# An mLSTM, mixture-of-experts and dense kernel on Trainium2: the tokens of the first three chunks are routed as one table

## The chip, the cores and the metric

The kernel runs on one core of a Trainium2 chip. The metric is device time in microseconds (us), the median of three runs. In the rows PE is the tensor engine, DVE the vector engine, ACT the scalar engine, POOL the GpSimd engine and SP the engine that issues most of the transfers.

## What is computed

Three layers in a row. The first is a gated recurrence over 768 steps for 4 batches and 8 heads of 40 columns. Its output is read as 3072 tokens of 320 columns. The second layer sends each token to the one of 8 experts with the largest logit and scales the expert's output by two gates. The third is a plain two-matrix layer. Cut to what matters:

```python
for t in range(S):                                     # attention, per batch and head
    m_new = np.maximum(f_gate[:, :, t] + m, i_gate[:, :, t])
    C = f_stab * C + i_stab * np.einsum('bhd,bhe->bhde', vt, kt)
    y[:, :, t] = o * h_tilde / denom
...
logits = x @ w_gate                                    # experts, x is (3072, 320)
e_idx = np.argmax(logits, axis=1)
gate_w = probs[np.arange(N), e_idx]
eom = 1.0 / (1.0 + np.exp(-(x @ w_output_gate)))
for e in range(E):
    mask = e_idx == e
    ye = np.maximum(x[mask] @ w1[e], 0.0) @ w2[e]
    out[mask] = gate_w[mask, None] * eom[mask, e, None] * ye
...
h = x @ w_in                                           # dense layer
g = np.maximum(0.01 * h, h)
return g @ w_out
```

## The kernel before

The recurrence is worked in chunks: 6 chunks of 128 steps by 4 batches give 24 units, unit c*4 + b. A hand-written loop (`for i in range(n_units)`) takes one unit further per iteration. The list `steps` (lines 426 to 441) sets what an iteration does and for which unit: an entry (lag, function) runs the function for unit i - lag. The order of this list is the order of the instructions on PE, ACT, DVE and POOL; each of these works its own queue strictly in that order.

The steps that matter here, with the names of the rows:

- `stage_d` (lag 0): PE makes the decay exponents pd (L278), ACT the exponentials pe (L287), four of eight from each of two PSUM banks. `stage_m` (lag 1): POOL masks pe to the lower triangle (L292).
- `stage_s` (lag 1): PE makes the scores psc (L317, 16 matmuls), DVE multiplies them with pe into ww (L324).
- `stage_o` (lag 2): PE makes pin (L338), the state update pu (L354) and ppv (L375); DVE makes the start of hh (L345), adds pu to the state st (L371), adds ppv to hh (L378) and makes the denominator from it (L382 to L384). `stage_g` (lag 3): POOL multiplies the output gate o with hh (L388) and masks the state into stm (L390). `stage_v` (lag 1): POOL scales v into wv (L306), not in the last chunk. `stage_y` (lag 3): DVE makes y (L402).
- `router.front` and `router.logits` (lag 5): PE transposes y (rt, L592), ACT copies it (xt, L594), PE multiplies with the two gates' weights (L602), ACT copies the 16 logits into the table lg (L603).
- `router.pick` (lag 6) works once per chunk, on the table of its four units: eight DVE operations (L629 to L636) find the largest logit and the one-hot oh. `router.rank` (lag 6) counts with small PE matmuls into the bank pp (L648, L649, L653) how many earlier tokens went to each expert, and ACT makes two exponentials (L660, L661). `router.place` (lag 7) makes from pp and the running count (both 8 numbers wide per unit) the slot sl of each token and its scale in the table meta: nine DVE operations (L671 to L683), ten for chunk 3 (L685).
- `router.scatter` (lag 0, last in the iteration): for a unit in the queue that `place` fills, POOL zeroes one number (gap, L696) and issues an indirect DMA (L697) that writes the unit's 128 rows of meta to the slots. Before the last chunk it takes one unit per iteration, in the last chunk four. When the last unit of chunk 3 has gone, the slots are loaded for the first half of the first expert (L1172), and POOL gathers its tokens (xr0a, L1014).

All eight PSUM banks come from one pool of eight, taken in turn. An iteration takes eight banks, rt, two pd, two psc, pin, pu and ppv, and a ninth, pp, where a table is ranked. A bank is taken by a new tile when the last reader of the old one is done.

At the end of iterations 5, 9, 13, 17 and 21 ACT opens the output gates of the next chunk with a sigmoid (L127), between two loads of its function table. Behind the loop the last units, chunks 4 and 5 of the table and the first expert's beginnings are interleaved by hand. Then come the experts and, from about 405 us on, the dense layer.

Of the kernel before, what the change touches and what calls it, by code (L numbers as in the profile page):

```python
# [10 lines left out]
F32 = mybir.dt.float32  # L11
F32R = mybir.dt.float32r
BF16 = mybir.dt.bfloat16
I32 = mybir.dt.int32
# [5 lines left out]
P = 128  # L20
B, H, S, D = 4, 8, 768, 40
BH = B * H
NC_ = S // P
DM = H * D
# [4 lines left out]
E = 8  # L29
# [8 lines left out]
NBIG = 3  # L38
CAPS = (CAP,) * (NBIG + 1) + (CAP - P,) * (E - NBIG - 1)
NOVER = 32  # L40
WARM = (11, 12, 7)
PW = 1024
SP = (mybir.EngineType.SP,)
# [11 lines left out]
def apart(tc, inst, before, why):  # L55

    for p in before:
        tc.declare_no_dep(inst.ins, p.ins, reason=why)
    before.append(inst)


def keep_warm(nc, psum, t, n):

    pt = psum.tile([P, 512], F32, tag="ps", name="warm")
    for _ in range(n):
        nc.tensor.matmul(pt, t[:, 0:P], t[:, 0:512], start=True, stop=True)
# [8 lines left out]
def attention(ctx, tc, qT, kT, k, v, i_gate, f_gate, o_gate, psum, ident, router, side, feed, fill):  # L75
    nc = tc.nc
    ctx.enter_context(tc.manual_schedule(engines=ORDERED))
    apool = ctx.enter_context(tc.tile_pool(name="apool", bufs=1))
    lpool = ctx.enter_context(tc.tile_pool(name="lpool", bufs=2))
    spool = ctx.enter_context(tc.tile_pool(name="spool", bufs=3))  # L80
    wpool = ctx.enter_context(tc.tile_pool(name="wpool", bufs=2))

    def ps(name):
# [64 lines left out]
    for j in range(3):  # L148
        nc.gpsimd.affine_select(
            sel, sel, pattern=[[-1, BH]], compare_op=ALU.not_equal, fill=1.0, base=-BH * j, channel_multiplier=1  # L150
        )

    m = apool.tile([BH, S], F32, name="m")
# [254 lines left out]
    for t in st:  # L408
# [4 lines left out]
        rowm, rowm, pattern=[[-D, 3]], compare_op=ALU.is_ge, fill=0.0, base=0, channel_multiplier=1  # L413
    )
    nc.gpsimd.affine_select(
        rowm, rowm, pattern=[[D, 3]], compare_op=ALU.is_ge, fill=0.0, base=D - 1, channel_multiplier=-1
# [3 lines left out]
    for i in range(3, AHEAD):  # L420
# [17 lines left out]
        (2, stage_o),  # L438
        (6, router.rank),
        (5, router.logits),  # L440
        (0, lambda c, b: router.scatter(B if c == NC_ - 1 else 1)),
    ]
    for i in range(n_units):
        for lag, fn in steps:
# [20 lines left out]
    a, b, c, d = units[-4:]  # L465
# [51 lines left out]
class Router:  # L517
# [39 lines left out]
    def setup(self):  # L557
        nc, cp = self.nc, self.cp
        self.tri = cp.tile([P, P], BF16, name="tri")
        nc.gpsimd.memset(self.tri, 1.0)  # L560
        nc.gpsimd.affine_select(
            self.tri, self.tri, pattern=[[1, P]], compare_op=ALU.is_gt, fill=0.0, base=0, channel_multiplier=-1
        )
        self.desc = cp.tile([P, E], F32, name="desc")
        nc.gpsimd.iota(
            self.desc, pattern=[[-REG, E]], base=E * REG, channel_multiplier=0, allow_small_or_imprecise_dtypes=True
        )
        self.meta = cp.tile([P, NC_, B, 4], I32, name="meta")
        nc.gpsimd.iota(self.meta, pattern=[[P, NC_], [S, B], [0, 4]], base=0, channel_multiplier=1)
        self.order.setup()  # L570

    def clear(self):
# [5 lines left out]
        ]  # L578

    def sink(self, c, b):  # L580
        if b == 0:
            self.lg[c] = self.rp.tile([P, B, 2 * E], F32, tag="lg", name=f"lg{c}")
        self.y[c, b] = self.rp.tile([P, DM], F32, tag="y", name=f"y{c}_{b}", bufs=4)
        return self.y[c, b].rearrange("p (h d) -> p h d", d=D)

    def front(self, c, b):
# [10 lines left out]
    def logits(self, c, b, copy=None):  # L597
        nc = self.nc
        pl = self.pl
        for kt in range(3):  # L600
            for t in HALVES:
                nc.tensor.matmul(pl[t], self.xt[:, kt, t], self.wg[:, kt], start=(kt == 0), stop=(kt == 2))  # L602
        (copy or nc.scalar.copy)(self.lg[c][:, b], pl)  # L603

    def span(self, c, b):

        if c == NC_ - 1:
            return {B // 2 - 1: (0, B // 2), B - 1: (B // 2, B // 2)}.get(b, (0, 0))
        return (0, B) if b == B - 1 else (0, 0)

    def t3(self, name, n, dt=F32):
        return self.rp.tile([P, B, E], dt, tag=name, name=name)[:, :n]

    def t2(self, name, n, dt=F32):
        return self.rp.tile([P, B], dt, tag=name, name=name)[:, :n]

    def pick(self, c, b):
        b0, n = self.span(c, b)
        if not n:
            return  # L620
        nc = self.nc
        lg = self.lg[c][:, b0 : b0 + n]
        g, og = lg[:, :, 0:E], lg[:, :, E : 2 * E]
        bc = lambda a: a[:, :, None].to_broadcast([P, n, E])
        desc = self.desc[:, None, :].to_broadcast([P, n, E])
        mx, eq = self.t2("mx", n), self.t3("eq", n)
        r, oh = self.t2("r", n), self.t3("oh", n, BF16)
        ex, zs = self.t3("ex", n), self.t2("zs", n)
        nc.vector.reduce_max(mx, g, axis=AX.X)  # L629
        nc.vector.tensor_tensor(eq, g, bc(mx), ALU.is_equal)  # L630
        nc.vector.tensor_mul(eq, eq, desc)
        nc.vector.reduce_max(r, eq, axis=AX.X)
        nc.vector.tensor_tensor(oh, desc, bc(r), ALU.is_equal)
        nc.vector.tensor_sub(ex, g, bc(mx))
        nc.vector.tensor_mul(eq, oh, og)
        nc.vector.reduce_sum(zs, eq, axis=AX.X)  # L636
        self.picked[c, b] = r, oh, ex, zs
# [25 lines left out]
    def place(self, c, b):  # L663
        b0, n = self.span(c, b)
        if not n:
            return
        nc = self.nc
        r, oh, ex, zs = self.picked.pop((c, b))
        pos, pr, se = self.t3("pos", n), self.t2("pr", n), self.t2("se", n)
        sl = self.t2("sl", n, I32)  # L670
        nc.vector.tensor_add(  # L671
            pos,
            self.pp[:, : n * E].rearrange("p (b e) -> p b e", e=E),
            self.base[:, None, :].to_broadcast([P, n, E]),
        )
        nc.vector.tensor_mul(pos, pos, oh)
        nc.vector.reduce_sum(pr, pos, axis=AX.X)
        nc.vector.scalar_tensor_tensor(sl, pr, float(E * REG), r, ALU.add, ALU.subtract)
        nc.vector.reduce_sum(se, ex, axis=AX.X)
        nc.vector.tensor_scalar(zs, zs, 1.0, None, ALU.add)  # L680
        nc.vector.scalar_tensor_tensor(se, se, 1e-9, zs, ALU.add, ALU.mult)
        nc.vector.reciprocal(self.meta[:, c, b0 : b0 + n, 2].bitcast(F32), se)
        nc.vector.tensor_add(self.base, self.base, self.pp[:, n * E : (n + 1) * E])  # L683
        if c == NC_ - 3:
            nc.vector.tensor_max(self.base, self.base, self.bump)  # L685
        self.queue += [(c, b0 + i, sl[:, i : i + 1]) for i in range(n)]

    def scatter(self, most=B):
        for c, b, sl in [self.queue.pop(0) for _ in range(min(most, len(self.queue)))]:
# [4 lines left out]
    def scatter_one(self, c, b, sl):  # L694
        nc = self.nc
        nc.gpsimd.memset(self.gap, 0)  # L696
        put = nc.gpsimd.indirect_dma_start(  # L697
            out=self.slots,
            out_offset=bass.IndirectOffsetOnAxis(ap=sl, axis=0),
            in_=self.meta[:, c, b, :],  # L700
            in_offset=None,
        )
        apart(self.tc, put, self.puts, "every token has a slot of its own")


class Order:


    def __init__(self, nc, pool):
# [6 lines left out]
        self.total = pool.tile([P, 1], I32, name="total")  # L716
        self.rows = pool.tile([P, NOVER], I32, name="rows")
        self.owner = pool.tile([P, NOVER], I32, name="owner")

# [30 lines left out]
    def past(self, pool):  # L750

        v = self.nc.vector
        wd = [P, NOVER, E]
        one = lambda nm: pool.tile([P, E], F32, name=nm, bufs=1)
        cap, nt, ends, ones = one("cap"), one("nt"), one("ends"), one("ones8")
        ni = pool.tile([P, E], I32, name="ni", bufs=1)
        steps = pool.tile([P, NOVER], F32, name="steps", bufs=1)
        d, ind, t = (pool.tile(wd, F32, name=nm, bufs=1) for nm in ("past_d", "past_i", "past_t"))

        def shares():  # L760
            self.nc.gpsimd.iota(
                steps, pattern=[[1, NOVER]], base=0, channel_multiplier=0, allow_small_or_imprecise_dtypes=True
            )
# [375 lines left out]
def mlstm_moe_mlp(  # L1139
# [48 lines left out]
    with ExitStack() as actx:  # L1188
# [39 lines left out]
        side += [nop] * 6 + parts  # L1228
        side += [nop, both(*acts[0:2]), acts[2], nop, acts[3], both(*acts[4:6]), acts[6]]
        attention(tc, qT, kT, k, v, i_gate, f_gate, o_gate, psum, ident, router, side, feed, fill)  # L1230
        load_slots(0, NJ // 2, NJ)

    wslot.append(ctx.enter_context(tc.tile_pool(name="wslot1", bufs=1)))
    with ExitStack() as mctx:
# [16 lines left out]
        loads = [w[0] for w in wide]  # L1251
        keep_warm(nc, psum, wts[0].w1h[:, 0], WARM[0])
        xs = ex.x(xr, "0b").all()
        for e in range(E):
# [63 lines left out]
            if e == E - 2:  # L1318
                more = nc.values_load(order.total[0:1, 0:1], min_val=0, max_val=NOVER)
            gs = []  # L1320
# [16 lines left out]

    keep_warm(nc, psum, wts[E].w1h[:, 0], WARM[1])
    with ExitStack() as octx:
# [21 lines left out]
    ctx.enter_context(tc.manual_schedule(engines=ORDERED))  # L1361
    keep_warm(nc, psum, wts[E].w1h[:, 0], WARM[2])
    for f in range(4):
# [98 lines left out]
```

## Time and profile before

| | us |
|---|---|
| median of three runs | 757.37 |
| the three runs | 756.65, 757.37, 759.11 |
| the profiled execution, its own time | 756.48 |
| its span | 754.8 |
| PE busy in the span | 720.6 (95%) |
| DVE, ACT, POOL busy | 461.5, 357.0, 353.2 |

The span is the time between the first and the last instruction of the profiled execution; the rest of its time lies around it. The busy times are sums over three layers with different limits, so they don't say what any one of them waits for.

### The profile page before, as it was taken

The numbers are of one execution on the slowest core, as the hardware profiler recorded it, in microseconds if no ns is written. First come the engines' busy times: TensorE is split into PE (matmuls) and PEld (weight loads), VectorE is DVE, ScalarE is ACT, GpSimd is POOL, SyncE is SP. The second block draws the span as 40 slices with busy tenths as digits, with TensorE's granted clock in tenths as the row PEclk, the third lists the DMA queues.
The fourth block names the chain that finished last, engine by engine and source line by source line (L and its number), as shares of the span: only waits on it lengthen the run. The fifth ranks groups of instructions, "written<-read, shape, count | busy, mean of one in ns | idle before, by whom it ended". The sixth has DMA issues, their size and how long they took to land.

```text
span 754.8 us, 14574 instructions
## 1 busy us (share of the span) xinstructions
PE 720.6 (95%) x5450; PEld 668.7 (89%) x5450; DVE 461.5 (61%) x925; ACT 357.0 (47%) x803; POOL 353.2 (47%) x396
## 2 busy tenths in 40 slices
PE   8888998899999999899998999999999999999998
PEld 6888998788879889799997988988988988988998
DVE  8989989674569889866764758048048038037020
ACT  5678776632562643554465355045045046046041
POOL 8757788754236473553322346046046036037041
PEclk9999999999999999999999999999999999999999
DMA  6887886411986766765762011001001000000000
GB/s 169 248 243 186 227 225 160 116 63 37 320 253 209 248 242 183 267 213 194 203 195 66 1 53 36 27 9 36 27 10 34 29 9 19 27 10 0 27 11 17
DMA packets 61791, 87.69 MB, mean 116 GB/s; under 512 B 8396, under 2 KB 53464, under 8 KB 60440
## 3 DMA queue, kind: packets, MB, share of 16 engines
q1 hardware_dynamic: 55928, 67.43, 30.2%
q10 hardware_dynamic: 2336, 10.75, 4.1%
q0 software_dynamic: 3456, 8.58, 3.5%
q8 instruction: 43, 0.70, 0.4%
q14 instruction: 28, 0.23, 0.1%
HBM read 67.87 MB, written 19.51 MB: 116 GB/s over the span
## 4 chain that ended last, share of the span: by engine, by line
PE 60%; DVE 11%; DMA 10%; issue 9%; POOL 5%; ACT 3%; POOLq 0%; SPq 0%; ACTq 0%; DVEq 0%
PE p L990 23%; PE po L1001 9%; PE po L999 9%; PE po L1000 9%; DMA xr<-xd,ms 7%; PE psc L317 4%; PE ppv L375 2%; POOL xr L1014 2%; DMA r<-in_moe_w_dram 2%; PE pd L278 1%; POOL x L1061 1%; PE pu L354 1%; PE rt L592 1%; DVE ww L324 1%; DVE w2l L907 1%
## 5 line engine op out<-in xcount | busy, mean ns | idle before, releaser
L1379 POOL TENSOR_TENSOR g2l<-lk,g2h 128x512 fp32r<-128x512 f32 (+1 forms) x112 | 126.6, 1133 | 213.7 <-ACT g2h L1378 203.7
L1388 DVE TENSOR_TENSOR lk<-p,lk 128x512 f32<-128x512 f32 (+1 forms) x112 | 68.9, 615 | 181.1 <-ACT lk L1387 179.1
L990 PE MATMUL p<-xhm,w1h 128*128 128x512 f32 (+1 forms) x336 | 119.5, 359 | 0.0
L990 PE MATMUL p<-xhm,w1l 128*128 128x512 f32 (+1 forms) x336 | 119.2, 359 | 0.0
L1001 PE MATMUL po<-w2h,g2l 128*128 128x320 f32 x384 | 118.7, 309 | 0.0
L1000 PE MATMUL po<-w2l,g2h 128*128 128x320 f32 x384 | 118.7, 309 | 0.0
L999 PE MATMUL po<-w2h,g2h 128*128 128x320 f32 x384 | 118.6, 309 | 0.0
L1387 ACT ACTIVATE lk<-p 128x512 f32<-128x512 f32 (+1 forms) x112 | 60.1, 536 | 73.7 <-PE p L990 73.7
L1061 POOL DMA_INDIRECT x<-yo,ms x26 | 32.1, 1236 | 104.0 <-ACT yo L1055 103.4
L990 PE MATMUL p<-xlm,w1h 128*128 128x512 f32 (+1 forms) x224 | 80.5, 359 | 0.1
L1000 PEld LDWEIGHTS po<-w2l,g2h 128*128 128x128 f32 x384 | 72.1, 188 | 0.2
L999 PEld LDWEIGHTS po<-w2h,g2h 128*128 128x128 f32 x384 | 72.1, 188 | 0.2
L1001 PEld LDWEIGHTS po<-w2h,g2l 128*128 128x128 f32 x384 | 72.1, 188 | 0.0
L1402 ACT COPY yo<-po 128x320 f32<-128x320 f32 x24 | 10.2, 426 | 130.7 <-PE po L1001 130.7
L990 PEld LDWEIGHTS p<-xhm,w1l 128*128 128x128 f32 x336 | 63.5, 189 | 9.4
L990 PEld LDWEIGHTS p<-xhm,w1h 128*128 128x128 f32 x336 | 63.4, 189 | 9.4
L1001 PE MATMUL po<-w2h,gl 128*128 128x320 f32 x208 | 64.9, 312 | 1.3 <-DVE gl L1041 1.3
L999 PE MATMUL po<-w2h,gh 128*128 128x320 f32 x208 | 65.4, 314 | 0.0
L1000 PE MATMUL po<-w2l,gh 128*128 128x320 f32 x208 | 64.7, 311 | 0.0
L1378 ACT CAST g2h<-lk 128x512 fp32r<-128x512 f32 (+1 forms) x112 | 61.6, 550 | 1.6 <-DVE lk L1388 1.6
L952 DVE STREAM_TRANSPOSE xtm<-x2r 32x384 f32<-32x384 f32 (+3 forms) x144 | 59.6, 414 | 2.8
L990 PE MATMUL ph<-xh,w1h 128*128 128x384 f32 (+1 forms) x168 | 60.8, 362 | 0.0
(251 smaller groups left out, 1597.9 us busy)
## 6 DMA issues: line engine op xcount, KB each, us to landing
r<-in_moe_w_dram SPq DMA_DIRECT2D x6, 1280.0 KB
r<-in_moe_w_dram SPq DMA_DIRECT2D x7, 1024.0 KB
raw<-in_moe_w_out_dram ACTq DMA_DIRECT2D x5, 1024.0 KB
r<-in_moe_w_dram SPq DMA_DIRECT2D x16, 256.0 KB
raw<-in_moe_w_in_dram ACTq DMA_DIRECT2D x4, 1024.0 KB
v<-in_v_dram SPq DMA_DIRECT2D x24, 164.0 KB
o<-in_o_gate_dram SPq DMA_DIRECT2D x6, 640.0 KB
k<-in_k_dram SPq DMA_DIRECT2D x24, 160.0 KB
```

The source lines that it names most:

```text
L317: nc.tensor.matmul(psc[:, j * P : (j + 1) * P], w["kTm"][:, h], w["qT"][:, h // 3], start=True, stop=True,)
L375: nc.tensor.matmul(ppv[t, h * VW : (h + 1) * VW], w["ww"][:, h, t], vb[:, h], start=True, stop=True)
L952: self.nc.vector.transpose(out=xt[f, k].rearrange("p k (j t) -> p k j t", t=P)[:, :, :, t], in_=blocks[t, :, g].rearrange("p j k f -> p k ...
L990: nc.tensor.matmul(ps, a, b, start=(i == 0), stop=(i == len(seq) - 1))
L999: nc.tensor.matmul(ps, gh[:, js], wh, start=(f == 0), stop=False)
L1000: nc.tensor.matmul(ps, gh[:, js], wl, start=False, stop=False)
L1001: nc.tensor.matmul(ps, gl[:, js], wh, start=False, stop=(f == n - 1))
L1061: put = self.nc.gpsimd.indirect_dma_start(out=self.x2, out_offset=bass.IndirectOffsetOnAxis(ap=ms[:, j, 1:2], axis=0), in_=yo, in_offset=None,
L1378: nc.scalar.copy(gh, lk)
L1379: nc.gpsimd.tensor_sub(gl, lk, gh.bitcast(F32))
L1387: nc.scalar.activation(lk, pf, AF.Copy, scale=0.01)
L1388: nc.vector.tensor_max(lk, pf, lk)
```

## The change

The new table GROUPED lists five groups of units: the twelve units of chunks 0 to 2, the four of chunk 3, the four of chunk 4, and two halves of chunk 5. `pick`, `rank` and `place` work once per group, when its last unit has come. So the calls for chunk 0 (i = 9 and 10) and chunk 1 (i = 13 and 14) are gone, and those at i = 17 and 18, where chunk 2 stood, work on twelve units. The number of scatters in an iteration is set anew too: one up to chunk 3, two in chunk 4's iterations (16 to 19), four in the last chunk's. The wide table and what is worked out from it have one buffer; y has three buffers for four, and the pool of hh two for three. The functions keep their code otherwise; lines move down by one to ten.

The diff, cut to its core:

```diff
+GROUPED = ((0, 3 * B), (3 * B, B), (4 * B, B), (5 * B, B // 2), (5 * B + B // 2, B // 2))
...
-    spool = ctx.enter_context(tc.tile_pool(name="spool", bufs=3))
+    spool = ctx.enter_context(tc.tile_pool(name="spool", bufs=2))
...
-        (0, lambda c, b: router.scatter(B if c == NC_ - 1 else 1)),
+        (0, lambda c, b: router.scatter({NC_ - 1: B, NC_ - 2: 2}.get(c, 1))),
...
-        self.meta = cp.tile([P, NC_, B, 4], I32, name="meta")
+        self.meta = cp.tile([P, NC_ * B, 4], I32, name="meta")
...
     def sink(self, c, b):
-        if b == 0:
-            self.lg[c] = self.rp.tile([P, B, 2 * E], F32, tag="lg", name=f"lg{c}")
-        self.y[c, b] = self.rp.tile([P, DM], F32, tag="y", name=f"y{c}_{b}", bufs=4)
+        b0, n = self.group(c, b)
+        if c * B + b == b0:
+            size = (B, 2) if n <= B else (n, 1)
+            self.lg[b0] = self.rp.tile([P, size[0], 2 * E], F32, tag=f"lg{size[0]}", name=f"lg{b0}", bufs=size[1])
+        self.y[c, b] = self.rp.tile([P, DM], F32, tag="y", name=f"y{c}_{b}", bufs=3)
...
+    def group(self, c, b):
+
+        for first, n in GROUPED:
+            if first <= c * B + b < first + n:
+                return first, n
 
     def span(self, c, b):
-
-        if c == NC_ - 1:
-            return {B // 2 - 1: (0, B // 2), B - 1: (B // 2, B // 2)}.get(b, (0, 0))
-        return (0, B) if b == B - 1 else (0, 0)
+        first, n = self.group(c, b)
+        return (first, n) if c * B + b == first + n - 1 else (0, 0)
 
     def t3(self, name, n, dt=F32):
-        return self.rp.tile([P, B, E], dt, tag=name, name=name)[:, :n]
+        m = max(n, B)
+        return self.rp.tile([P, m, E], dt, tag=f"{name}{m}", name=name, bufs=2 if m == B else 1)[:, :n]
...
-        lg = self.lg[c][:, b0 : b0 + n]
+        lg = self.lg[b0][:, 0:n]
...
-        self.queue += [(c, b0 + i, sl[:, i : i + 1]) for i in range(n)]
+        self.queue += [((b0 + i) // B, (b0 + i) % B, sl[:, i : i + 1]) for i in range(n)]
```

How this moves instructions is shown at two places. In these rows a number behind a name tells its buffer, and the brackets what an instruction waits for. The first place is DVE's queue in iteration 9, from the denominators to ww. Before:

```order
L384 RECIPROCAL ppv_2_1009<-ppv_2_1009 128x8
L629 TENSOR_REDUCE mx<-lg_489 128x4
L630 TENSOR_TENSOR eq<-lg_489,mx 128x32
L631 TENSOR_TENSOR eq<-eq,desc 128x32
L632 TENSOR_REDUCE r<-eq 128x4
L633 TENSOR_TENSOR oh<-desc,r 128x32
L634 TENSOR_TENSOR ex<-lg_489,mx 128x32
L635 TENSOR_TENSOR eq<-oh,lg_489 128x32
L636 TENSOR_REDUCE zs<-eq 128x4
L324 TENSOR_TENSOR ww_0_1097<-psc_0_0_1098,pe_0_955 128x512
L324 TENSOR_TENSOR ww_0_1097<-psc_0_1_1104,pe_0_955 128x512
```

After, where the lines have moved down by one:

```order
L385 RECIPROCAL ppv_2_1008<-ppv_2_1008 128x8
L325 TENSOR_TENSOR ww_0_1082<-psc_0_0_1083,pe_0_954 128x512
L325 TENSOR_TENSOR ww_0_1082<-psc_0_1_1089,pe_0_954 128x512
L403 TENSOR_TENSOR y_2_1095<-o_354,ppv_2_1008 128x320
L346 TENSOR_TENSOR hh_3_1097<-pin_3_1098,eT 128x328
L372 TENSOR_TENSOR st_198<-st_198,pu_3_1103 120x246
```

The eight operations of the pick are gone from between the denominators of one unit and ww of the next.

The second place is POOL's queue in iteration 21, from the product of the gate with hh on. Before:

```order
L388 TENSOR_TENSOR o_1744<-o_1744,hh_2_2348 128x320 [waits DVE_49]
L390 TENSOR_TENSOR stm_201<-st_197,rowm 120x369 [waits PE_49]
L292 AFFINE_SELECT pe_1_2422<-pe_1_2422 128x1024 [waits Activation_49]
L388 TENSOR_TENSOR o_1744<-o_1744,hh_3_2459 128x320 [waits DVE_49]
L390 TENSOR_TENSOR stm_202<-st_198,rowm 120x369 [waits PE_49]
```

After:

```order
L389 TENSOR_TENSOR o_1656<-o_1656,hh_2_2274 128x320 [waits DVE_49]
L391 TENSOR_TENSOR stm_201<-st_197,rowm 120x369 [waits PE_49]
L706 MEMSET gap 1x1 [waits Pool_49]
L707 DMA slots<-meta,sl 28672x4 [waits DMASW0_49]
L706 MEMSET gap 1x1 [waits Pool_49]
L707 DMA slots<-meta,sl 28672x4 [waits DMASW1_49]
L706 MEMSET gap 1x1 [waits Pool_49]
L707 DMA slots<-meta,sl 28672x4 [waits DMASW2_49]
L706 MEMSET gap 1x1 [waits Pool_49]
L707 DMA slots<-meta,sl 28672x4 [waits DMASW3_49]
L293 AFFINE_SELECT pe_1_2352<-pe_1_2352 128x1024 [waits Activation_49]
L389 TENSOR_TENSOR o_1656<-o_1656,hh_3_2389 128x320 [waits DVE_49]
```

Four scatters, each with its memset, now stand between the state's mask stm of iteration 21 and the mask of pe in iteration 22, where there was none.

## Rows read from the trace of the kernel before

A row of a timeline gives the start in us, the duration in us, the engine, the line and operation, what is written from what, the shapes, the number of instructions in it, and in brackets the idle time of the engine before it with what ended it. Where a window cuts a group of matmuls, the number is that of the part inside. A row of the windows view gives the stretch, its length, the busy time of PE, PEld (weight loads), DVE, ACT and POOL with the number of instructions of each, PE's granted clock as a share of the full one, the busy share of the DMA engines and GB/s.

**Rows 1.** Chain of waits, 128 to 215 us: start, us, what.

```profile
176.96 1.13 DMA slots<-meta,sl
```

**Rows 2.** Timeline of PE, starts of psc (L317) in seven iterations.

```profile
57.79 0.89 PE L317 MATMUL psc<-qTm,kTm 128*128 128x128 f32 x6
...
73.57 0.70 PE L317 MATMUL psc<-qTm,kTm 128*128 128x128 f32 x2
...
84.61 1.11 PE L317 MATMUL psc<-qTm,kTm 128*128 128x128 f32 x8
...
98.80 2.00 PE L317 MATMUL psc<-qTm,kTm 128*128 128x128 f32 x16
...
104.19 1.00 PE L317 MATMUL psc<-qTm,kTm 128*128 128x128 f32 x7
...
130.75 1.00 PE L317 MATMUL psc<-qTm,kTm 128*128 128x128 f32 x7
...
137.43 0.78 PE L317 MATMUL psc<-qTm,kTm 128*128 128x128 f32 x5
```

**Rows 3.** Timeline of DVE: the first pick, its place, the tail.

```profile
58.30 2.37 DVE L631 TENSOR_TENSOR eq<-eq,desc 128x32 f32<-128x32 f32 x1
...
69.05 0.13 DVE L683 TENSOR_TENSOR count<-count,pp 128x8 f32<-128x8 f32 x1
...
160.24 0.19 DVE L631 TENSOR_TENSOR eq<-eq,desc 128x32 f32<-128x32 f32 x1
```

**Rows 4.** Timeline of POOL beside that pick.

```profile
58.27 2.35 POOL L907 TENSOR_TENSOR w1l<-r,w1h 128x1024 fp32r<-128x1024 f32 x1 [4.47 <-ACT w1h L890]
```

**Rows 5.** Timelines of ACT and PE at i = 10.

```profile
67.94 2.17 ACT L287 ACTIVATE pe<-pd,gT 128x128 f32<-128x128 f32 x8
...
69.33 0.80 PE L354 MATMUL pu<-wv,k 128*120 128x123 f32 x6 [2.26 <-DVE count L683]
70.06 1.44 PE L375 MATMUL ppv<-v,ww 128*64 128x41 f32 x32
```

**Rows 6.** Timelines of ACT and PE at i = 14.

```profile
94.42 2.17 ACT L287 ACTIVATE pe<-pd,gT 128x128 f32<-128x128 f32 x8
...
95.85 0.80 PE L354 MATMUL pu<-wv,k 128*120 128x123 f32 x6
```

**Rows 7.** Timeline of PE: rank at 17, pu at 18.

```profile
113.81 0.26 PE L648 MATMUL pp<-oh,ones 128*128 128x8 bf16 x4
...
114.10 0.53 PE L602 MATMUL rt<-wg,xt 128*64 128x16 f32 x12
...
120.87 0.80 PE L354 MATMUL pu<-wv,k 128*120 128x123 f32 x6 [2.42 <-ACT pe L287]
```

**Rows 8.** Timeline of POOL, iterations 20 to 23: scatters, masks, products.

```profile
133.71 1.01 POOL L697 DMA_INDIRECT slots<-meta,sl  x1 [0.16 <-issue]
...
136.00 1.10 POOL L292 TENSOR_SCALAR_AFFINE_SELECT pe<-pe 128x1024 f32<-128x1024 f32 x1
...
142.67 0.81 POOL L388 TENSOR_TENSOR o<-o,hh 128x320 f32<-128x320 f32 x1 [1.88 <-DVE hh L378]
...
145.11 1.01 POOL L697 DMA_INDIRECT slots<-meta,sl  x1 [0.86 <-DVE count L685]
...
148.96 0.96 POOL L697 DMA_INDIRECT slots<-meta,sl  x1 [0.22 <-issue]
149.94 1.10 POOL L292 TENSOR_SCALAR_AFFINE_SELECT pe<-pe 128x1024 f32<-128x1024 f32 x1
```

**Rows 9.** Timeline of DVE, hh in iterations 20, 21 and 22.

```profile
136.63 0.49 DVE L378 TENSOR_TENSOR hh<-hh,ppv 128x328 f32<-128x328 f32 x1 [1.82 <-PE rt L592]
...
142.09 0.49 DVE L378 TENSOR_TENSOR hh<-hh,ppv 128x328 f32<-128x328 f32 x1
...
150.86 0.49 DVE L378 TENSOR_TENSOR hh<-hh,ppv 128x328 f32<-128x328 f32 x1 [3.75 <-PE pd L278]
```

**Rows 10.** Window over the four scatters: busy times, PE clock, DMA share.

```profile
145.00:151.00 6.00, 4.47 (x67) 3.34 (x65) 2.25 (x6) 4.11 (x12) 5.21 (x8) 1.00 0.02 1
```

More of the change, by code (lines that the diff above doesn't have):

```diff
@@ L567, in setup @@
         )
-        self.meta = cp.tile([P, NC_, B, 4], I32, name="meta")
-        nc.gpsimd.iota(self.meta, pattern=[[P, NC_], [S, B], [0, 4]], base=0, channel_multiplier=1)
+        self.meta = cp.tile([P, NC_ * B, 4], I32, name="meta")
+        nc.gpsimd.iota(self.meta.rearrange("p (c b) w -> p c b w", b=B), pattern=[[P, NC_], [S, B], [0, 4]], base=0, channel_multiplier=1)
         self.order.setup()
@@ L602, in logits @@
                 nc.tensor.matmul(pl[t], self.xt[:, kt, t], self.wg[:, kt], start=(kt == 0), stop=(kt == 2))
-        (copy or nc.scalar.copy)(self.lg[c][:, b], pl)
+        b0 = self.group(c, b)[0]
+        (copy or nc.scalar.copy)(self.lg[b0][:, c * B + b - b0], pl)
+    def group(self, c, b):
+        for first, n in GROUPED:
+            if first <= c * B + b < first + n:
+                return first, n
     def span(self, c, b):
-        if c == NC_ - 1:
-            return {B // 2 - 1: (0, B // 2), B - 1: (B // 2, B // 2)}.get(b, (0, 0))
-        return (0, B) if b == B - 1 else (0, 0)
+        first, n = self.group(c, b)
+        return (first, n) if c * B + b == first + n - 1 else (0, 0)
     def t3(self, name, n, dt=F32):
-        return self.rp.tile([P, B, E], dt, tag=name, name=name)[:, :n]
+        m = max(n, B)
+        return self.rp.tile([P, m, E], dt, tag=f"{name}{m}", name=name, bufs=2 if m == B else 1)[:, :n]
     def t2(self, name, n, dt=F32):
-        return self.rp.tile([P, B], dt, tag=name, name=name)[:, :n]
+        m = max(n, B)
+        return self.rp.tile([P, m], dt, tag=f"{name}{m}", name=name, bufs=2 if m == B else 1)[:, :n]
     def pick(self, c, b):
@@ L681, in place @@
         nc.vector.scalar_tensor_tensor(se, se, 1e-9, zs, ALU.add, ALU.mult)
-        nc.vector.reciprocal(self.meta[:, c, b0 : b0 + n, 2].bitcast(F32), se)
+        nc.vector.reciprocal(self.meta[:, b0 : b0 + n, 2].bitcast(F32), se)
         nc.vector.tensor_add(self.base, self.base, self.pp[:, n * E : (n + 1) * E])
@@ L699, in scatter_one @@
             out_offset=bass.IndirectOffsetOnAxis(ap=sl, axis=0),
-            in_=self.meta[:, c, b, :],
+            in_=self.meta[:, c * B + b, :],
             in_offset=None,
```

## The prediction

> **What bounds the kernel now.** I read the page first. PE is busy for nearly all of the span, but that is a mean over stages. From 405 us on, a plain dense layer keeps PE full, and the change does not reach it. So I went to the timeline of the attention part (50 to 165 us) and to the chain of waits behind it. There the reader should see two things. First, in the chain the end of attention is followed by the last scatters into the token table, by the load of that table and by the gathers of the first expert, one after the other [rows 1]. Nothing runs ahead of this, so a microsecond lost or won before the last scatter is taken to reach the end whole. Second, the start of the scores (psc, L317) marks each of the 24 iterations. An undisturbed one takes 104.19 - 98.80 = 5.39 us on PE. The two from 57.79 to 73.57 take 15.78 and the two from 84.61 to 98.80 take 14.19 [rows 2]: 5.0 and 3.4 us more than four undisturbed ones. These are the places where chunk 0 and chunk 1 are picked and placed, and 8.4 us is all that the change can win there.
>
> **What is removed: the picks and places of chunks 0 and 1.** That is 34 VectorE instructions and sixteen small matmuls, moved into one wide table. The pick is dear at i = 9 because of one operation: L631 takes 2.37 us there and 0.19 where nothing disturbs it [rows 3], and it lies over a GpSimd operation that ends with it [rows 4]. The Trainium skill has a rule for this (SBUF — State Buffer, section "Who interferes with whom"): a VectorE operation with two SBUF inputs and a reading GpSimd operation exclude each other for the whole instruction. The trace agrees with 2.37 against 2.35 us. By that rule alone one would book the 2.2 us as a gain; I do not, for the reason in the next sentences.
>
> At i = 10, PE's pu (L354) waited 2.26 us for the place's last operation, count L683, whose read frees the PSUM bank; ppv followed at 70.06 [rows 3, 5]. Afterwards no place holds a bank. But ppv takes the bank that the first four exponentials of pe set free, and pe begins at 67.94 behind the sigmoid of the next gate with its two table loads [rows 5]. Half of its 2.17 is done at 69.0; ACT starts some 0.3 earlier without the rank ahead of the logits, so 68.75. Gain 70.06 - 68.75 = **1.3**, with bounds 0 and 5.0 [rows 2].
>
> At i = 14 the same two releasers stand even closer: pe begins at 94.42, half done at 95.5, and pu ran at 95.85 [rows 6]. With ACT 0.3 to 0.6 earlier the gain lies between 0 and 1.5, since PE was not late for one reason only; I take **0.8**.
>
> **What is added: a table of twelve units at i = 17.** The rank has 24 matmuls in a row instead of 8. The 8 took 114.10 - 113.81 = 0.29 us, so 24 take 0.87, and the 0.58 delays the logits and the chain on ACT behind them, for which PE then waits (2.42 us, on pe) [rows 7]. Loss **0.6**; from 0.3, if the shared weights make them cheaper, to 1.2 with wider columns. The 17 operations of pick and place become three times as wide. Between 0.19 us for 32 elements [rows 3] and 0.49 for 328 (hh at 142.09) [rows 9] a line gives 1.0 ns an element, 0.065 more each, 1.1 in all. That lies on VectorE, which at both places runs ahead of the chain on ACT, so nothing is booked for it; without that cover it is 1.1. The buffers that shrink (hh from 3 to 2, y from 4 to 3, one wide table) are each read one to two iterations after they are written, and no reader is passed: nothing.
>
> **What is moved: eight scatters, to the end of attention.** This is the term that decides. Before, iterations 10 to 19 hold one scatter each, 20 two, 21 none, 22 four. Now 10 to 17 hold none, 18 and 19 two, and 20, 21 and 22 four each. A scatter (gap memset and indirect DMA) takes GpSimd's queue for 1.28 us when others follow (145.11 to 148.96 in three steps) [rows 8]. Behind it in that queue stands the mask L292 of the next iteration, which ww on VectorE needs, then L388 and L390. The single scatters cost nothing that shows: 98.80 to 104.19 has one in it. So the eight that leave give nothing back.
>
> The bursts cost in two ways. The queue itself: the pair ran from 133.71 until the mask at 136.00, the four from 145.11 to 149.94, 4.83 us [rows 8]. And what waits for PE comes late while a burst runs. The hh addition L378 waited 1.82 us and began 0.63 behind the pair, and 3.75 us and began 0.92 behind the four [rows 9]. The releasers that these rows name, rt and pd, are not its operand, which is ppv, ahead of them on PE. The trace gives no cause for it, but it is so at both bursts.
>
> In the times of before: at i = 20 four scatters end at 133.71 + 4.83 = 138.54 instead of 136.00. hh starts at about 139.3 instead of 136.63, 2.7 late. Then L388 at 139.85, and L388 and L390 together 1.6 (142.67 until the 0.86 of waiting ahead of 145.11) [rows 8] to 141.4. There the new four of i = 21 begin, to 146.3. hh of that iteration, at 142.09 before [rows 9], starts at 147.2: 5.1 late. The place of chunk 3 stands behind it and releases the last four, which move from 145.11 to 150.2. Loss **5.1**. By GpSimd's queue alone (mask 1.10, L388 and L390 1.6, four scatters 4.83, mask, L388 and L390 again, counted from 138.54) those four begin at 148.8, and the loss is 3.7: the lower bound. The pair at i = 19 replaces a single one. A single costs nothing, the pair at i = 20 cost 1.29 of PE's time (psc followed 130.75 at 137.43 instead of after 5.39, at 136.14) [rows 2]; I take half, **0.65**, and nothing for the pair at i = 18, where PE waits for ACT anyway.
>
> **Sum:** -1.3 - 0.8 + 0.6 + 0.65 + 5.1 = +4.25 us. The profiled execution took 756.48 us, of it 754.8 in the span; with the sum it is 760.7. The runs' median is 757.37, 0.9 above it, and that is what will be compared: 757.37 + 4.25 = **761.6**. A measurement of this kernel tells about 0.3% from no change, 2.3 us: the line for slower is 759.6, for faster 755.1.
>
> **The rivals.** (a) *The gains win.* If the place and the pick were the whole cause of the excess at i = 9 to 11 and 13 to 15, all 8.4 us come back, against 3.7 for the queue and 0.6 for the rank: 753.3. For it: pu waited for count alone by the trace [rows 5]. Against it: pe on ACT ends right beside it at both places [rows 5, 6]. It decides at 4.3 us of gain: with more, the kernel is no slower. Chance 0.14.
> (b) *The queue alone.* The late hh was something else that happened beside the bursts, and only the order in GpSimd's queue counts: 3.7 - 1.5 = +2.2, so 759.6, right on the line. For it: no wait in the trace names the scatters. Chance 0.22.
> (c) *Every burst stalls.* The pairs at i = 18 and 19 each cost the 1.82 us that hh waited at the other pair [rows 9]: 5.1 + 3.6 - 1.5 = +7.2, so 764.6. For it: both bursts of before did so. Against it: at 18 PE has another wait in that place. Chance 0.13.
> A variant of (c) is PE's clock. In the stretch of the four scatters PE was busy 4.47 of 6 us and the granted clock stayed at 1.00, 2.4 GHz [rows 10]; with longer waits it could fall to 1.2 GHz, and the sixteen psc matmuls of 2.00 [rows 2] would take up to 2 us more per burst. The Trainium skill (TensorE: Matmul & The Clock Gate, section "HAM oscillation — how this bites in real kernels") says that waiting for data lowers the clock again and again; by it this variant would come at every burst, 6 us on top. The row at the burst speaks against it, so it is only the tail of (c), 0.02 of its 0.13.
> That the change does not do what it says can be left out: the order shows the instructions where it says, and all 24 scatters.
>
> **How the numbers follow.** My forecast has 0.51: 761.6, from 759.8 (the queue's 3.7, larger gains) to 763.5. Rivals 0.14, 0.22, 0.13. The range takes in the forecast and (b) whole, and of (a) and (c) what lies near: 755.5 to 765.3, which leaves out about 0.16. Faster: (a), 0.14. Within 0.3%: half of (b) and 0.05 of the forecast's lower end, 0.16. Slower: the rest, 0.70.
>
> **What the changed profile would show.** Right: psc from i = 9 to 11 some 1.3 us shorter, with ppv waiting for pe; hh of i = 20 and i = 21 waiting about 3 to 5 us until the bursts end; the last four scatters of attention's loop 3 to 5 us later than 145.11, and the first expert by as much. Wrong: if hh does not wait in the burst of i = 21, (b) holds; if scores at i = 11 begin 3 us or more earlier, the gains were put too low; if the last scatters are late but the first expert is not, the chain behind attention has slack that I did not see.

## The result, and the profile after

The changed kernel took 765.22 us (median of 4 runs, 762.82 to 766.75), the kernel before beside it 757.01: a ratio of 1.0101, 95% interval 1.0067 to 1.0135. It is slower by 8.2 us where 4.25 was forecast, and 0.1 us inside the upper end of the range. The profiled execution took 762.82 us, its span 761.1 against 754.8.

First the gains, in the timeline of PE in the changed kernel, one stretch in each fence (start and duration in us, engine, line, operation, out<-in, count, and in brackets the idle time before and what ended it). Lines are one to ten higher than before, so pu is L355, ppv L376, the rank L658 to L663.

```profile
68.50 1.13 PE L376 MATMUL ppv<-v,ww 128*64 128x41 f32 x32 [2.31 <-ACT pe L288]
```

```profile
111.94 0.46 PE L658 MATMUL pp<-oh,ones 128*128 128x8 bf16 x12
...
112.68 0.53 PE L605 MATMUL rt<-wg,xt 128*64 128x16 f32 x12
...
118.98 0.80 PE L355 MATMUL pu<-wv,k 128*120 128x123 f32 x6 [2.03 <-ACT pe L288]
```

At i = 10 ppv starts at 68.50 and waits for pe, where pu waited for the place before [rows 5]; the sum had put it at 68.75. The rank of twelve units takes 112.68 - 111.94 = 0.74 us against 0.29 [rows 7], and pu of i = 18 still waits 2.03 us for pe.

Then the burst. POOL's timeline, iterations 20 to 23 (scatters L707, mask L293), answers [rows 8]:

```profile
132.40 1.01 POOL L707 DMA_INDIRECT slots<-meta,sl  x1 [0.15 <-issue]
...
136.25 0.96 POOL L707 DMA_INDIRECT slots<-meta,sl  x1 [0.21 <-issue]
137.22 1.11 POOL L293 TENSOR_SCALAR_AFFINE_SELECT pe<-pe 128x1024 f32<-128x1024 f32 x1
...
140.04 1.01 POOL L707 DMA_INDIRECT slots<-meta,sl  x1 [0.17 <-issue]
...
144.85 1.11 POOL L293 TENSOR_SCALAR_AFFINE_SELECT pe<-pe 128x1024 f32<-128x1024 f32 x1
...
149.07 1.01 POOL L707 DMA_INDIRECT slots<-meta,sl  x1 [0.86 <-DVE count L695]
...
153.89 1.11 POOL L293 TENSOR_SCALAR_AFFINE_SELECT pe<-pe 128x1024 f32<-128x1024 f32 x1
```

Three bursts of four now follow one another, with 2.6 and 3.3 us between them, and the last four start at 149.07 instead of 145.11. On DVE and PE the same stretch shows waits that no queue explains. DVE's hh (L379), which answers [rows 9], and pieces of PE's ppv under the last burst:

```profile
136.71 0.49 DVE L379 TENSOR_TENSOR hh<-hh,ppv 128x328 f32<-128x328 f32 x1 [3.38 <-remote]
...
146.04 0.50 DVE L379 TENSOR_TENSOR hh<-hh,ppv 128x328 f32<-128x328 f32 x1 [1.11 <-PE ppv L376]
```

```profile
151.97 0.33 PE L376 MATMUL ppv<-v,ww 128*64 128x41 f32 x3 [0.39 <-issue]
152.71 0.20 PE L376 MATMUL ppv<-v,ww 128*64 128x41 f32 x1 [0.41 <-issue]
153.44 0.23 PE L376 MATMUL ppv<-v,ww 128*64 128x41 f32 x1 [0.53 <-issue]
```

hh of i = 20 waits 3.38 us for something the profile calls remote, and PE issues ppv one to three matmuls at a time with gaps of 0.4 to 0.5 us that are put down to nothing. This looked like the late hh of the prediction, only longer.

### The profile page after: what moved, and what is told of

Same layout as the page of the kernel before. It is cut to its first block, busy times and chain, and to the rows that moved or that the text cites. A ratio compares the mean times of both kernels' runs of the same rounds, so it can differ in the third digit from the quotient of the medians.

```text
span 761.1 us, 14537 instructions
## 1 busy us (share of the span) xinstructions
PE 722.0 (95%) x5450; PEld 670.1 (88%) x5450; DVE 449.2 (59%) x891; ACT 356.9 (47%) x799; POOL 352.8 (46%) x396
```

## The experiments

All kernels below were run in later sets, each beside the kernel before; ratios are to that. The kernel before itself had medians of 760.8, 760.2 and 761.1 us there, with single runs from 756 to 765, so a profile is one draw from that spread and only ratios with intervals carry a verdict. In the diffs "router.scatter" is the last entry of `steps`.

**The moved scatters alone.** The kernel before with the schedule of the change; the tile of the slots, sl, has four buffers, so that three chunks can wait for their scatters.

```diff
-        (0, lambda c, b: router.scatter(B if c == NC_ - 1 else 1)),
+        (0, lambda c, b: router.scatter(B if c == NC_ - 1 else 2 if c * B + b >= 18 else 0)),
```

> The kernel before with one part of the change alone: its scatters are held back and issued as in the changed kernel (two in iterations 18 and 19, four in 20, 21 and 22). The tables stay one per chunk. Between the starts of psc in iteration 19 and in the tail the changed kernel took 40.1 us where the kernel before took 30.2, 9.9 more. If the moved scatters cause the loss, this kernel loses about as much with nothing gained in front of it: 757 + 9.9, some 766 to 767. If the wide table or the smaller buffers cause it, it stays near 757.

Measured: 1.0029 (1.0002 to 1.0056), 2.2 us with bounds of 0.2 and 4.3. A loss is there without the wide table, but smaller than expected, and its form is another. DVE's waits between 118 and 165 us (sum, count, longest), and POOL's bursts:

```profile
DVE ww L324 <- POOL pe L292: 13.0, 4, 4.5
DVE hh L378 <- PE ppv L375: 0.5, 1, 0.5
```

```profile
135.44 1.01 POOL L697 DMA_INDIRECT slots<-meta,sl  x1 [0.16 <-issue]
...
143.07 1.01 POOL L697 DMA_INDIRECT slots<-meta,sl  x1 [0.16 <-issue]
...
150.69 1.01 POOL L697 DMA_INDIRECT slots<-meta,sl  x1 [0.16 <-issue]
```

ww waits 13.0 us for the mask that stands behind the scatters, hh waits 0.5 in all. No engine issues late under a burst. The last four scatters start at 150.69. The late hh did not come back with the bursts that were to cause it.

**The queue without a transfer.** The kernel before with memsets of a spare tile in POOL's queue, as many as the change adds scatters.

```diff
-        (0, lambda c, b: router.scatter(B if c == NC_ - 1 else 1)),
+        (0, lambda c, b: (router.scatter(B if c == NC_ - 1 else 1), router.fillers({18: 1, 19: 1, 20: 2, 21: 4}.get(c * B + b, 0)))),
...
+    def fillers(self, n):
+        for _ in range(6 * n):
+            self.nc.gpsimd.memset(self.idle, 0.0)
```

> The kernel before with its own scatters, and in GpSimd's queue as much extra work without any transfer as the change adds in scatters: memsets of a spare tile, six of about 0.2 us for one scatter, one such filler in iterations 18 and 19, two in 20, four in 21. If only the place in GpSimd's queue counts, this costs what the moved scatters cost, 757 + 8 to 10. If the scatters themselves hold up the other engines beside that, it costs only the queue's part, 3.7 in the sum of the prediction: some 760.7; and VectorE's hh then waits for no burst.

Measured: 1.0057 (1.0037 to 1.0078), no less than the scatters themselves; the two intervals overlap. POOL, and DVE's waits from 118 to 170 us:

```profile
144.57 6.23 POOL L697 MEMSET idle<- 128x128 f32 x24
...
153.56 1.02 POOL L702 DMA_INDIRECT slots<-meta,sl  x1 [0.16 <-DVE y L402]
```

```profile
DVE ww L324 <- POOL pe L292: 17.1, 5, 4.5
```

24 memsets take 6.23 us where four scatters take 5.1: a filler is 0.28 us longer than what it stands for, some 2.2 us over eight of them, and the last four scatters come 2.9 us later than in the run above. Work in the queue costs what scatters cost; no transfer is needed. That speaks against the late hh as the cause.

**The pair of iteration 20 taken apart.** The kernel before with one scatter in 20 and one in 21.

```diff
-        (0, lambda c, b: router.scatter(B if c == NC_ - 1 else 1)),
+        (0, lambda c, b: router.scatter(B if c * B + b >= 22 else 1)),
```

> The kernel before with the pair of scatters at iteration 20 taken apart: one in 20, one in 21. GpSimd does the same work. If two scatters back to back hold up what waits for PE (hh waited 1.82 us behind the pair), 1.3 us come back: 755.7. If only the queue counts, GpSimd gets no less to do and the time stays at 757.

Measured: 0.9957 (0.9936 to 0.9979), faster than the kernel before by about 3 us, more than either theory gave. The second profile of the kernel before, below, shows where it comes from.

**No two scatters in a row.** The changed kernel with three scatters in each of 18 to 21, spread between POOL's other work.

```diff
         (1, stage_m),
+        (0, lambda c, b: router.scatter(1 if c * B + b >= 18 else 0)),
...
+        if 18 <= c * B + b + 3 < n_units:      # in stage_g, between o*hh and stm
+            router.scatter(1)
...
-        (0, lambda c, b: router.scatter({NC_ - 1: B, NC_ - 2: 2}.get(c, 1))),
+        (0, lambda c, b: router.scatter(2 if c * B + b == 22 else 1)),
```

> The changed kernel with the same twelve scatters in iterations 18 to 21, but three in each and never two in a row: one behind the mask, one between the products o*hh and stm, one at the end (and four in 22, two of them in a row). If it takes scatters in a row to hold up the other engines, the late hh goes and only the queue's part stays: 765.2 - 6 = 759. If each scatter costs by itself, or only the queue counts, it stays within 1.5 of 765.

Measured: 1.0056 (1.0039 to 1.0073), as slow as the change. It is the amount in the queue, not the row of scatters.

**Both kernels again.** Unchanged, for profiles beside each other.

> The kernel before, unchanged, for a second profile beside the next three. The profiles of the four kernels so far show no late hh behind any burst, while the first profiles of both kernels do. If scatters in a row hold up what waits for PE, hh (L378) waits here again about 1.8 us behind the pair of iteration 20 and 3.7 behind the four of 22. If only the place in GpSimd's queue counts, hh waits for nothing there, and ww waits for the mask behind the four.

> The changed kernel, unchanged, a second profile. By the queue alone: ww waits for the mask L293 in iterations 21 to 23 for 10 to 15 us in all, hh for no burst, the first gather of tokens comes some 5 to 7 us later than in the kernel before, and the time is 5 to 8 above it. By the late hh: hh waits 1 to 4 us behind each burst as in the first profile, and the masks are not what ww waits for.

Measured: the change 1.0044 (1.0022 to 1.0067). In the second profile of the kernel before hh waits for no burst. DVE's pick at i = 21 and POOL beside it:

```profile
136.20 2.32 DVE L630 TENSOR_TENSOR eq<-lg,mx 128x32 f32<-128x32 f32 x1
138.56 1.00 DVE L631 TENSOR_TENSOR eq<-eq,desc 128x32 f32<-128x32 f32 x1
```

```profile
136.90 0.81 POOL L388 TENSOR_TENSOR o<-o,hh 128x320 f32<-128x320 f32 x1
137.67 0.80 POOL L390 TENSOR_TENSOR stm<-st,rowm 120x369 f32<-120x369 f32 x1
138.42 1.09 POOL L292 TENSOR_SCALAR_AFFINE_SELECT pe<-pe 128x1024 f32<-128x1024 f32 x1
```

L630, 0.19 us where nothing disturbs it, takes 2.32 and ends at 138.52, with POOL's stm (138.47); L631 takes 1.00 and ends with the mask. Behind a pair of scatters POOL's o*hh, stm and mask come 1.3 us later, and so fall upon the pick. With the pair taken apart the same rows read:

```profile
135.91 1.06 DVE L630 TENSOR_TENSOR eq<-lg,mx 128x32 f32<-128x32 f32 x1
137.00 0.19 DVE L631 TENSOR_TENSOR eq<-eq,desc 128x32 f32<-128x32 f32 x1
```

```profile
135.35 0.81 POOL L388 TENSOR_TENSOR o<-o,hh 128x320 f32<-128x320 f32 x1
136.11 0.79 POOL L390 TENSOR_TENSOR stm<-st,rowm 120x369 f32<-120x369 f32 x1
```

L630 takes 1.06, L631 0.19, and the last four scatters start at 143.47 instead of 145.84. That is most of the gain of the run with singles: 1.3 us in the queue had cost 2.1 on DVE, and of the 3.7 us between the two profiles 2.2 lie between psc of i = 19 and the last four.

The changed kernel shows the same lock twice, and longer. DVE's pick and place of chunk 3, and POOL beside them:

```profile
137.20 3.05 DVE L643 TENSOR_TENSOR oh<-desc,r 128x32 bf16<-128x32 f32 x1
...
144.79 3.04 DVE L688 SCALAR_TENSOR_TENSOR sl<-pr,r 128x4 int32<-128x4 f32 x1
```

```profile
137.57 1.10 POOL L293 TENSOR_SCALAR_AFFINE_SELECT pe<-pe 128x1024 f32<-128x1024 f32 x1
138.63 0.81 POOL L389 TENSOR_TENSOR o<-o,hh 128x320 f32<-128x320 f32 x1
139.39 0.80 POOL L391 TENSOR_TENSOR stm<-st,rowm 120x369 f32<-120x369 f32 x1
...
145.20 1.10 POOL L293 TENSOR_SCALAR_AFFINE_SELECT pe<-pe 128x1024 f32<-128x1024 f32 x1
146.25 0.81 POOL L389 TENSOR_TENSOR o<-o,hh 128x320 f32<-128x320 f32 x1
147.02 0.79 POOL L391 TENSOR_TENSOR stm<-st,rowm 120x369 f32<-120x369 f32 x1
```

L643 ends at 140.25 with stm (140.19), L688 at 147.83 with the next stm (147.81): each stood still while mask, o*hh and stm ran through, three POOL instructions in a row. The rule of the Trainium skill (SBUF — State Buffer, section "Who interferes with whom") that a VectorE operation with two SBUF inputs and a reading GpSimd operation exclude each other is borne out, and here the block lasts over three GpSimd instructions, 3.05 us, not one. By the records L643 and L688 had begun 0.4 us ahead of the mask; why they did not end in that time is not shown. In the third profile of the changed kernel, below, L688 falls beside scatters and takes 0.16:

```profile
147.26 0.16 DVE L688 SCALAR_TENSOR_TENSOR sl<-pr,r 128x4 int32<-128x4 f32 x1
```

**POOL relieved.** The changed kernel with wv and stm made on DVE from iteration 18 on.

```diff
-            nc.gpsimd.tensor_mul(
+            (nc.vector if c * B + b + 1 >= 18 else nc.gpsimd).tensor_mul(
                 wv, w["v"], wT[:, c, w["hs"]][:, :, None].to_broadcast([P, H, VW])
...
-            nc.gpsimd.tensor_mul(
+            (nc.vector if c * B + b + 3 >= 18 else nc.gpsimd).tensor_mul(
                 stm[b], st[b], rowm[:, None, :, None].to_broadcast([3 * D, 3, 3, VW])
```

> The changed kernel, its scatters where they are, but from iteration 18 on the products wv (0.73 us) and stm (0.80) are made on VectorE instead of GpSimd: 1.5 us less in GpSimd's queue in 18 and 19, 0.8 in 20 to 22, 5.4 in all. If GpSimd's queue is what binds there, the first gather and the end come 3 to 5 us earlier than in the changed kernel, though VectorE has that much more to do. If the scatters cost by themselves, nothing comes back, or VectorE's added 2 to 3 us make it slower.

Measured: 1.0031 (1.0010 to 1.0051), not told apart from the change, and less than expected.

```profile
126.03 1.94 DVE L307 TENSOR_TENSOR wv<-v,wT 128x328 f32<-128x328 f32 x1
```

```profile
130.92 0.81 POOL L389 TENSOR_TENSOR o<-o,hh 128x320 f32<-128x320 f32 x1 [3.32 <-DVE hh L379]
...
147.57 1.31 POOL L707 DMA_INDIRECT slots<-meta,sl  x1 [1.32 <-DVE count L693]
```

DVE now holds the work: wv takes 1.94 there beside POOL's mask, hh is late, and POOL waits 3.32 us for it at 130.92. The last four scatters start at 147.57, 24.11 us behind psc of i = 19 against 24.92 in the changed kernel. So the two engines seem to share the bound in these iterations: moving work from one to the other did not lift it.

**Two chunks instead of three.**

```diff
-GROUPED = ((0, 3 * B), (3 * B, B), (4 * B, B), (5 * B, B // 2), (5 * B + B // 2, B // 2))
+GROUPED = ((0, 2 * B), (2 * B, B), (3 * B, B), (4 * B, B), (5 * B, B // 2), (5 * B + B // 2, B // 2))
...
-        (0, lambda c, b: router.scatter({NC_ - 1: B, NC_ - 2: 2}.get(c, 1))),
+        (0, lambda c, b: router.scatter({14: 2, 18: 2, 20: 2, 21: 2, 22: 4, 23: 4}.get(c * B + b, 1))),
```

> The change with a group of two chunks instead of three: eight units picked at 13 and placed at 14, chunk 2 by itself as before. Twelve scatters then have the iterations 14 to 21: 2, 1, 1, 1, 2, 1, 2, 2. By the queue the crowding is gone (GpSimd's extra load against the kernel before is one scatter at 18 and two at 21), and the time is that of the kernel before within 2 us. If the wide table by itself costs (its rank in a row, its operations), it stays 3 or more above the kernel before.

Measured: 1.0001 (0.9975 to 1.0028). With twelve scatters over eight iterations the loss is gone. From psc of 9 to psc of 17 this kernel took 51.53 us and from 17 to 19 it took 16.49, together 0.1 more than the second profile of the kernel before (table below): what the wide table gains it also costs.

**The mask ahead of the gather.** Behind the loop, in both: the kernel with singles, and the changed kernel.

```diff
-    fill.gather()
-    router.front(*z)
     stage_m(*d)
     stage_g(*b)
+    fill.gather()
+    router.front(*z)
     stage_s(*d)
```

> The kernel before with the pair at iteration 20 taken apart (one scatter in 20, one in 21) and, behind the loop, the last mask and o*hh issued on GpSimd ahead of the first gather instead of behind it. In the second profile of the kernel before that mask stood 4.0 us behind the gather, which waited for the slots' load, and ww waited 4.8 us for it; PE then ran 10 us at half its clock. If the queue behind that wait is what sets the end of attention, 2 to 5 us come back: a ratio of 0.993 to 0.996 with the pair's part. If the gather's data bind anyway, only the pair's part shows, 0.997 to 1.

> The changed kernel with the last mask and o*hh ahead of the first gather. The late gather of the changed kernel then holds up less behind it. If its loss went on through that mask, 2 to 4 us of it come back and the ratio falls from 1.0044 to 1.000 to 1.002; if the loss goes on through the gather's own data, it stays at 1.003 or more.

Measured: 0.9953 (0.9932 to 0.9974) and 1.0041 (1.0017 to 1.0065), the same as without it. DVE then waits for the gathered tokens (the changed kernel, 114 to 172 us):

```profile
DVE xr0a L942 <- DMA xr0a<-xd,ms: 3.3, 1, 3.3
```

So the end of attention seems to go through the gather's data, and through the scatters that let it start. The kernel with singles, 0.9957, is the version that beats both.

**Both kernels a third time.**

> The kernel before, a third profile. By the queue alone: hh waits for no burst, ww waits for the mask behind the four scatters and behind the gather, 6 to 8 us in all. By the late hh of the first profile: 1.8 and 3.7 us at hh.

> The changed kernel, a third profile. By the queue: ww waits 8 us or more for masks, the last four scatters of the loop come 2.5 to 4 us later than in the kernel before beside it, PE's half clock in the tail lasts as long or longer, and the ratio is 1.004 to 1.008. By the late hh: hh waits behind each burst, and the ratio is near 1.010 as in the first comparison.

Measured: 1.0048 (1.0024 to 1.0072). DVE's waits in the two, from 114 to 170 us:

```profile
DVE ww L324 <- POOL pe L292: 8.2, 2, 5.5
DVE hh L378 <- PE ppv L375: 0.3, 1, 0.3
```

```profile
DVE ww L325 <- POOL pe L293: 14.2, 4, 5.5
DVE hh L379 <- PE ppv L376: 1.8, 2, 1.4
```

In the first fence (kernel before) ww waits 8.2 us for masks, in the second (changed) 14.2. Here the lag of the queue shows as waits for the mask, in the profile above as locked operations; from psc of 19 to the last four the price is the same within 0.2 us, as the table below shows.

## Where the time went

Starts read from the timelines of three pairs of profiles, as before / after, us. "Last four" is the first of the four scatters of chunk 3.

| stretch | first pair | second pair | third pair |
|---|---|---|---|
| start to psc of i = 9 | 57.79 / 56.52 | 56.60 / 57.12 | 56.39 / 61.67 |
| psc of 9 to psc of 17 | 51.79 / 50.50 | 53.27 / 50.43 | 53.20 / 48.83 |
| psc of 17 to psc of 19 | 15.78 / 15.12 | 14.62 / 16.23 | 14.72 / 16.83 |
| psc of 19 to last four | 19.75 / 26.93 | 21.35 / 24.92 | 21.26 / 25.03 |
| of it, to the first scatter of 20 | 8.35 / 10.26 | 9.06 / 8.20 | 8.97 / 9.79 |
| of it, from there to last four | 11.40 / 16.67 | 12.29 / 16.72 | 12.29 / 15.24 |
| last four to first gather | 9.44 / 9.44 | 10.70 / 11.77 | 11.36 / 11.43 |
| first gather to last scatter | 22.41 / 24.55 | 23.78 / 25.97 | 24.89 / 24.01 |
| last scatter to the end | 577.84 / 578.04 | 578.08 / 577.56 | 579.08 / 577.80 |

In each pair the last stretch is the same within 1.3 us: what is lost ahead of it reaches the end whole. The third pair's changed kernel lost 5.3 us ahead of the first pick, with PE granted 1.2 GHz from 52 to 58 us; five other profiles with these tables have 56.5 to 57.3 there, so this is not the change.

## Why the prediction was right, and where it was not

**The decision** was right: the moved scatters cost more than the removed picks and places gain, and all of it reaches the end. The number was not: the later ratios, 1.0044 and 1.0048, are 3.3 and 3.7 us, the first is 8.2, and that 765.22 fell inside a range ending at 765.3 is luck. Between the first comparison and the later ones it is the kernel before that moved (757.0, then 760.2 and 761.1); the changed kernel took 765.2, 764.3 and 764.6. What made the kernel before faster in the first stays open.

The signs that the prediction named point both ways. In the first profile the last four came 4.0 us later and so did the first gather, as put, but hh waited 3.38 us at i = 20 and only 1.11 at i = 21; in the later ones it waits for no burst, which was the sign for (b).

**The gains** (1.3 and 0.8, together 2.1 us from i = 9 to 17) measured 1.3, 2.8 and 4.4. The mechanism stood as put: ppv and pe, not the place, set these iterations. Split at psc of i = 12 (79.22 / 77.74, 79.51 / 78.27, 79.22 / 81.24), the gain around chunk 1 is 1.1 in each pair. That around chunk 0 is 0.2, 1.8 and 3.3, and goes with something that the prediction did not look at, PE's granted clock. From 60 to 80 us, where pu or ppv waits some 2.3 us, its mean was 0.91, 0.83 and 0.83 before and 0.91, 0.91 and 1.00 in the changed kernel. The third pair, before and changed (behind POOL the granted clock, the DMA share, GB/s):

```profile
60.00:80.00 20.00, 17.16 (x228) 16.32 (x225) 16.64 (x46) 14.02 (x39) 15.00 (x19) 0.83 0.78 214
```

```profile
60.00:80.00 20.00, 16.93 (x271) 16.30 (x267) 12.90 (x33) 16.25 (x45) 13.88 (x14) 1.00 0.72 217
```

So the size of this gain is not the change's alone.

**The table of twelve** (0.6) cost 1.6 and 2.1 in the later pairs, and the first was 0.7 shorter; from 108 to 128 us the granted clock was 0.91 and 1.00 there, 0.91 and 0.91 in the second pair, 0.91 and 0.89 in the third. The rank by itself was sized well, 0.45 us more. The rest was left out: in i = 17 of the second pair PE took 7.28 us against 5.80. That with the banks of the places gone the rotation moves, so that the copy of the logits and pe stand in PE's way, is argued and not tried, and neither are the smaller buffers. The twelve units are not needed for it: the kernel with two chunks, whose table at 17 has four, took 16.49 us from 17 to 19, at a clock of 0.83. This is one mis-sized term. Gains and table together leave 2.0, 1.2 and 2.3 us, near the 1.5 of the sum, which is luck.

**The crowded scatters** (5.75 with the pair at 19). By themselves they measured 2.2 us, at most 4.3 (1.0029): the queue's 3.7 fits that, 5.1 does not. The pairs of profiles had 7.2, 3.6 and 3.8 from psc of 19 to the last four. The step that was mis-sized is the one that priced the bursts by the late hh of [rows 9]. It took a wait without a cause, seen at two bursts of one profile, for a property of the kernel. In twelve later profiles no wait of hh is over 1.5 us and none is put down to remote (what is left of late issue is one transpose of PE, rt, 2.20 and 1.65 us in the two of the changed kernel); fillers without a transfer cost no less than scatters, and spreading the scatters gives nothing back.

What gave DVE and PE those waits in the first pair of profiles stays open; there they did happen, in both kernels. They do not explain 7.2 against 3.6. Of that difference, 2.8 us lie ahead of the first burst of four (table). There hh did wait 1.15 us behind the changed kernel's pair at 19, and psc of 20 followed 7.05 us behind psc of 19; but in the third pair it followed 6.83 behind with no such wait. The other 0.8 is the kernel before, which was shorter in the first pair (11.40 against 12.29), although its hh waited 1.82. From the first scatter of 20 to the last four the sum gives 16.5 us with the late hh and 15.1 by the queue. The changed kernel took 16.7 with it, 16.7 without it, where the lock held the place back, and 15.2 in the third pair, where POOL waits for no other engine in between. That 3.6 and 3.8 meet the bound of 3.7 is in part chance: they also hold the pair at 19 and the lock in the kernel before.

Inside the queue's part one thing was overlooked too: the price is paid not only where ww waits for the mask but where POOL's reading operations are pushed onto the pick and the place. The prediction named the lock only at i = 9, and booked nothing for it.

**The chain behind attention** was taken to pass the delay whole. It did, and in two pairs added to it: from the first gather to the last scatter 2.1 us more in the first, and in the second 1.1 ahead of the gather and 2.2 behind it. Windows from 158 to 180 us, kernel before and changed kernel of the second pair (after DVE, ACT and POOL the granted clock, the DMA share, GB/s):

```profile
158.00:180.00 22.00, 18.95 (x187) 17.62 (x187) 16.68 (x83) 6.06 (x20) 11.61 (x19) 0.77 0.18 55
```

```profile
158.00:180.00 22.00, 17.52 (x180) 15.82 (x176) 11.60 (x52) 4.30 (x14) 9.73 (x15) 0.61 0.17 54
```

While the gather is awaited PE idles, and the clock that it is granted falls to 1.2 GHz for much of the tail: a mean of 0.77 before, 0.61 after. PE's wait for the gathered tokens in these two:

```profile
PE px0a L939 <- DMA xr0a<-xd,ms: 3.7, 2, 2.7
```

```profile
PE px0a L949 <- DMA xr0a<-xd,ms: 3.9, 2, 3.2
```

In the first pair, whose last scores come later, PE did not wait for them and the clock was 1.00 and 0.98, so the price differs from run to run. The prediction did not look for a lower clock here. The Trainium skill (TensorE: Matmul & The Clock Gate, section "HAM oscillation — how this bites in real kernels") says that waiting for data lowers the clock again; in this tail the trace agrees. The tail is longer in the second pair, but not in the third (24.89 and 24.01), so the clock's share in the loss is not settled. Over whole runs the median granted clock was 0.975 for the kernel before in both later sets, 0.9725 and 0.971 for the changed kernel.

Under the bursts, where [rows 10] showed none, the changed kernel does have a lower clock: the variant of (c), given 0.02, came about. From 134 to 152 us the mean was 1.00 in all three profiles of the kernel before and 0.91, 0.81 and 0.91 in the changed one, each time behind a wait of PE (3.69, 2.20 and 1.65 us); the sixteen psc matmuls that follow took 3.27, 3.73 and 3.41 us instead of 2.00. The second pair, before and changed, and its psc:

```profile
134.00:152.00 18.00, 16.84 (x290) 16.20 (x287) 14.22 (x44) 12.26 (x35) 12.36 (x19) 1.00 0.38 90
```

```profile
134.00:152.00 18.00, 14.80 (x194) 14.26 (x191) 17.15 (x45) 10.65 (x29) 15.34 (x25) 0.81 0.47 99
```

```profile
144.86 3.73 PE L318 MATMUL psc<-qTm,kTm 128*128 128x128 f32 x16
```

No loss of its own is shown for it: in the third pair POOL's queue is full up to the last four all the same.

**Rivals.** (a) fell: the kernel was slower in all three comparisons. The one gain that reaches the 4.3 us (4.4, third pair) stands beside a clock of 0.83 before against 1.00, and the table's term takes 2.1 of it back. (b), the queue alone, holds in mechanism for the two later pairs; their 1.0044 and 1.0048 are some 3.5 us, with the clock, the lock and the table's cost beside the 2.2 that it gave. (c) has the size of the first comparison; there hh waited behind the pair at 19 but not behind the one at 18, and the later profiles do not bear it out.

## What to carry to other kernels

Work moved later into an in-order queue is to be costed by what that queue still has to do before the next hand-over, iteration by iteration; the sum of other engines' savings says little about it. A wait that the profile gives no cause for should be seen in a second profile before a term is built on it, and stretches of two kernels should be compared with their granted clocks beside them. And where two engines block each other's operations, a delay of one moves its work onto the other's: look at what it will then stand beside.

## What was not expected of the hardware

A vector operation on 128x4 numbers (L688, 0.16 us beside scatters) took 3.04 us because three POOL operations ran through without letting it in. A pair of scatters in one iteration instead of one in each cost about 3 us (0.9957). And the same instructions behind attention ran at a mean granted clock of 1.00, 0.77 and 0.69 in three profiles of the kernel before (158 to 180 us), with 22.41, 23.78 and 24.89 us from the first gather to the last scatter; in the first PE did not wait for the gathered tokens, in the others 3.7 and 4.1 us. That this decides was not tried.
